# A fused attention, MoE and MLP kernel: the x sums of the first MoE pass made in eight parts during attention and parked in DRAM

## The chip, the cores and the metric

The kernel runs on one core of a Trainium2 chip. The time is the device time of one execution in microseconds (us). A core has a matrix engine (PE), three element-wise engines (DVE, ACT, POOL), a sequencer that issues transfers (SP), and 16 DMA engines that all transfers of the kernel share. The on-chip memory of a core is SBUF; matmul results go to eight banks of PSUM.

## The reference

Three stages follow each other. Batch B=4, heads H=8, 512 local and 32 global tokens per batch, head size 64, so x has 2304 rows of 512.

```python
s_ll = where(|i - j| <= 32, q_l @ k_l.T / sqrt(64), -1e9)     # local tokens: a window
a_l  = softmax(concat([q_l @ k_g.T / sqrt(64), s_ll]))        # and the 32 global ones
out_l = a_l @ concat([v_g, v_l])
out_g = softmax(q_g @ concat([k_g, k_l]).T / sqrt(64)) @ concat([v_g, v_l])
x = heads side by side                                        # [2304, 512]

P = exp(x @ w_gate - max)                                     # [2304, 8]
8 times: P /= P.sum(1); P /= P.sum(0); P *= 2304 / 8          # Sinkhorn
y = sum over 8 experts e of  P[:, e] * (relu(x @ w1[e]) @ w2[e])   # 512 -> 1024 -> 512

z = elu(y @ w_in) @ w_out                                     # 512 -> 2048 -> 512
```

## The kernel before

**Arithmetic.** Each fp32 product is three matmuls on rounded halves: high by high, low by high, high by low (`three`, L110). So every operand exists as a pair, with h and l at the end of its name: the high part is a cast (mostly on ACT), the low part the difference (on DVE or POOL).

**Attention.** The loop `for t in range(nq + 2)` (L527) goes over 32 heads, four steps `i` each. Head t is loaded two heads ahead (`load`: kq on SP, L184), split by `prep` (kh on ACT L210, sq and kl on POOL), scored (`s`), exponentiated on ACT (`e`, L254), transposed (`ptp`, copied to `pt`) and multiplied with the values (`o`, L317); DVE copies `o` to `os` (L337), which frees the bank that the next head's `o` needs. Global scores are `sg` (L275), global values `pg`/`og`. Every fourth head 256 columns of x are transposed into the x operands, and from t=21 on `x_out` (L390) writes the pair `xdh`, `xdl` of a batch to DRAM, 1 MB each.

**Filler.** Between the steps PE runs matmuls of a generator, `fill`: gate logits (`lgp`, `lgt`) and the MoE units 0 and 1 on the first 1024 tokens, in plain form (L112 to L121: `m1` products, `hh` by ACT, `hl` by DVE, then `m2` products added into `acc`). Their raw weights are loaded at L458 and split at L104 and L108. Where the filler isn't ready there are `idle` matmuls during the first eight heads (L493).

**First MoE pass.** A unit is half an expert, 16 in all. After the loop the rest of `fill` is worked off in a loop at L1020, and then units 2 to 15 run over the first 1024 tokens. `mix1` makes its products with seven block products `q1` to `q7` in place of eight (`PROD`): they multiply blocks x11, x12, x21, x22 of x and sums s1 to s4 of these with blocks and sums `wt1` to `wt4` of the weights. `mix2` multiplies the result with the second weights and adds it, times P, into eight `acc` tiles. The block x21 lies in the tile `xs4` (named s4 in the code) until unit 1 has used it last; then the sum s4 goes there. `sums_of_x` makes s1 to s4 on POOL, DVE and ACT, a step at every fifth step of the loop at L1020, followed by the load of unit 2's weights (`w1r`, L725) and its first weight sums (`build[:9]`).

**Sinkhorn** is a queue `timed` of nine small pieces, of which `passed(ns)` starts the next one when the matmuls issued since the last are worth its due time. A round is eight DVE instructions (L852 to L845) around one tiny PE matmul `pcs` (L850), which waits for DVE's `cs`. P (`pr`) is first needed at the first finished tile of unit 2's `mix2`; the sums of units 0 and 1 in `acc` are multiplied by P there (L1002, on ACT, eight tiles in a block).

**Order.** All engines work off their own list in the order in which the code issues. A transfer is issued by SP in that order too, and waits there for its source and its destination.

Of the kernel before, what the change touches and what calls it, by code (L numbers as in the profile page):

```python
# [50 lines left out]
def tile_net(ctx: ExitStack, tc, kq, vw, vc, qg, wg, w1, w2, wi, wo, consts, out):  # L51
# [16 lines left out]
    xd = {p: dram.tile([128, 4, TP[1]], F32, tag="xd" + p, name="xd" + p) for p in "hl"}  # L68
    sd = {p: dram.tile([128, 4, 2, HALF], F32, tag="sd" + p, name="sd" + p) for p in "hl"}
    yd = dram.tile([128, TP[0] // 128, D], F32, tag="yd", name="yd")  # L70
    wd = {
# [380 lines left out]
    def load_unit(u):  # L452

        raw = []
        for i in range(10):
# [6 lines left out]
            yield  # L462

    def ready(b):
        while not st.get(("xready", b)):
            yield "wait"
# [11 lines left out]
    with tc.manual_schedule():  # L478
# [46 lines left out]
        prep(0)  # L525
        unit0_weights = load_unit(0)
        for t in range(nq + 2):  # L527
            if t + 2 < nq:
# [11 lines left out]
            for i in range(4):  # L540
# [20 lines left out]
                if i >= 2:  # L561
                    between = scores_g(t, i - 2) if t < nq else iter(())
                    if 0 <= t - 1 < nq:
                        pv(t - 1, i - 2, between)
                    for _ in between:
                        pass
# [9 lines left out]
                if i == 3 and t < nq:  # L576
                    fill_for(FILL)
                    st["gq"] = t

# [6 lines left out]
                if i == 2 and t >= 5 and (t - 5) % 4 == 0:  # L586
                    fill_for(FILL)
                    x_t((t - 5) // 4)
                    if ((t - 5) // 4) % 2 == 1:
                        st["xready", (t - 5) // 8] = True  # L590
                        if (t - 5) // 8 >= 2:
                            x_out((t - 5) // 8)
                if t == 3 * H + 2 and i % 2 == 0:
                    logits_part(2)
        x_tg()
        x_out(B)
        for b in (B - 1, B):
            for _ in range(2):
                logits_part(b)
                for _ in range(9):  # L600
                    next(fill, None)
# [7 lines left out]
    sm = mright.enter_context(tc.tile_pool(name="sm", bufs=1, side="right", reuse_waits="tile"))  # L609
    psum = ctx.enter_context(tc.tile_pool(name="psum", bufs=8, space=PSUM))  # L610

# [10 lines left out]
    def raw_tile(shape, dt, name):  # L622
        r = rawm.tile([128, 2 * HALF], F32, tag="raw", name=name)
        n = int(np.prod(shape))
        v = r[:, :n].bitcast(dt)
        return v.rearrange("p (a f) -> p a f", a=shape[0])

    def second_x(names):
# [10 lines left out]
    def sums_ahead(c):  # L639
# [35 lines left out]
        return [lambda: load("h"), lambda: load("l")], [whole, first, hi, lo]  # L675

    def sums_of_x(m):

        v = {}

        def blk(n, q):
            return xop[n + q][:, :, :m]

        def whole(n, src, eng):
            v[n] = raw_tile((2, m), F32, "x" + n)
            eng.tensor_tensor(out=v[n], in0=blk(src, "h").bitcast(F32), in1=blk(src, "l").bitcast(F32), op=ALU.add)

        def comb(dst, a, b, op, buf):
            nc.vector.tensor_tensor(out=v[buf], in0=v[a], in1=v[b], op=op)
            v[dst] = v[buf]  # L690

        def hi(n):
            nc.scalar.copy(blk(n, "h"), v[n])

        def lo(n, eng=nc.vector):
            eng.tensor_tensor(out=blk(n, "l"), in0=v[n], in1=blk(n, "h").bitcast(F32), op=ALU.subtract)


        eng = nc.gpsimd
        return [  # L700
            lambda: whole("21", "s4", nc.gpsimd),
            lambda: whole("22", "22", nc.vector),
            lambda: comb("s1", "21", "22", ALU.add, "22"),
            lambda: hi("s1"),
            lambda: whole("11", "11", nc.gpsimd),
            lambda: lo("s1", eng),
            lambda: comb("s3", "11", "21", ALU.subtract, "21"),
            lambda: comb("s2", "s1", "11", ALU.subtract, "22"),
            lambda: hi("s2"),
            lambda: hi("s3"),  # L710
            lambda: lo("s2", eng),
            lambda: lo("s3"),
            lambda: whole("12", "12", nc.vector),
            lambda: comb("s4", "12", "s2", ALU.subtract, "12"),
            lambda: hi("s4"),
            lambda: lo("s4"),
        ]

# [225 lines left out]
    def mix2(p, u, i, fcs):  # L944

        if i not in open2:
            open2[i] = [psum.tile([128, 512], F32, tag="b", name="m2"), 0]
        ps, n = open2[i]
        for fc in fcs:
            t = slice(i * 128, i * 128 + 128)  # L950
# [40 lines left out]
    def mix2_all(p, u, last):  # L991
# [7 lines left out]
        rest += [(i, range(4)) for i in range(tiles) if i not in seen]  # L999
        if u == 2 and p == 0:  # L1000
            for i in range(tiles):
                nc.scalar.mul(accs[i], accs[i], pr[:, i, 0:1])  # L1002
        for i, f in pre:
# [8 lines left out]
    with tc.manual_schedule():  # L1012
        conv = deque(range(8 * U2))
        timed.extend(sinkhorn())
        sums = sums_of_x(SL)
        first, build = weights1(2, nc.gpsimd)

        pre = deque(sums[:-2] + first + build[:9])
        steps = 0
        for r in fill:  # L1020
# [3 lines left out]
            passed(r if isinstance(r, float) else 0.0)  # L1024
        pop(pre, len(pre))
        for f in build[9:13]:
            f()
        order = [(0, u) for u in range(2, U1)] + [(1, u) for u in range(U1)]
        nload, nbuild = weights2(2)
        side1.extend(build[13:] + sums[-2:] + nload)  # L1030
        for a, (p, u) in enumerate(order):
# [216 lines left out]
```

## Time and profile before

| | |
|---|---|
| median of 3 runs | 2011.51 us (2010.76 to 2012.47) |
| profiled execution: its own time | 2012.67 us |
| profiled execution: span of the profile | 2010.9 us |
| mean granted PE clock | 0.996 of full |
| busy: PE, DVE, ACT, POOL | 99%, 69%, 37%, 36% |

The 1.77 us between the profiled execution's time and its span lie outside of the program. The attention loop ends at about 256 us, the first product of unit 2 starts at 292.18 us, and from 330 us on PE is busy without a break almost to the end.

### The profile page before, as it was taken

To read this page: it belongs to the slowest core of one execution; us is meant where nothing else is said; L and a number is where in the kernel's file an instruction comes from. 1 tells how busy PE (TensorE), PEld (TensorE's weight loads), DVE (VectorE), ACT (ScalarE), POOL (GpSimd) and SP (SyncE) were. 2 spreads that over 40 slices of the span, in tenths; PEclk is the share of its full clock that TensorE was granted. 3 is DMA by queue.
4 is the path that set the end of the run, shared out by engine and by line. 5 is a ranking of instruction groups with operands and counts; after the bars stand their busy time and mean duration, and the time that the engine had idled before them with its cause. 6 is when DMAs were issued, how large, how long until landed. Compare 5 with 4: busy or idle time off the path is not lost.

```text
span 2010.9 us, 29132 instructions
## 1 busy us (share of the span) xinstructions
PE 1989.8 (99%) x11051; PEld 1739.3 (86%) x11051; DVE 1382.8 (69%) x2531; ACT 752.9 (37%) x1488; POOL 725.9 (36%) x612
## 2 busy tenths in 40 slices
PE   8999999999999999999999999999999999999999
PEld 7998977888888888899999999999999988887997
DVE  6766667677677767777788888888867654445444
ACT  6655524233333323333333333333333233433333
POOL 6554442232243323323344444444423212322222
PEclk9999999999999999999999999999999999999999
DMA  7435331223322232441132232232212140202001
GB/s 230 138 121 160 101 105 53 63 66 103 115 87 90 75 103 85 159 176 63 58 107 93 90 104 85 92 96 86 85 64 73 44 178 1 84 3 81 1 32 58
DMA packets 65628, 181.43 MB, mean 90 GB/s; under 512 B 6608, under 2 KB 16592, under 8 KB 63440
## 3 DMA queue, kind: packets, MB, share of 16 engines
q1 hardware_dynamic: 65488, 179.57, 27.4%
q8 instruction: 87, 1.43, 0.3%
q14 instruction: 53, 0.43, 0.1%
HBM read 146.77 MB, written 32.77 MB: 89 GB/s over the span
## 4 chain that ended last, share of the span: by engine, by line
PE 89%; DVE 4%; ACT 4%; issue 1%; DMA 1%; POOL 0%; SPq 0%; ACTq 0%; DVEq 0%; POOLq 0%
PE m L116 16%; PE m L112 16%; PE m L114 16%; PE q L925 10%; PE q L924 10%; PE q L923 10%; PE o L317 2%; DVE eg L133 2%; PE m L1157 1%; PE m L1156 1%; PE m L1159 1%; PE ptp L300 1%; ACT eg L131 1%; ACT er L132 1%; ACT er L130 1%
## 5 line engine op out<-in xcount | busy, mean ns | idle before, releaser
L116 PE MATMUL m<-w2h,hl 128*128 128x512 f32 x1088 | 428.1, 394 | 2.4 <-DVE hl L121 2.4
L114 PE MATMUL m<-w2l,hh 128*128 128x512 f32 x1088 | 427.6, 393 | 0.0
L112 PE MATMUL m<-w2h,hh 128*128 128x512 f32 x1088 | 427.4, 393 | 0.0
L895 ACT ACTIVATE hh<-t 128x288 fp32r<-128x288 f32 (+1 forms) x368 | 184.9, 502 | 445.5 <-DVE t L892 445.4
L897 DVE SCALAR_TENSOR_TENSOR hl<-t,hh 128x288 fp32r<-128x288 f32 (+1 forms) x368 | 276.4, 751 | 4.0 <-ACT hh L895 0.3
L962 DVE SCALAR_TENSOR_TENSOR acc<-m,pr,acc 128x512 f32<-128x512 f32 x247 | 183.6, 747 | 134.5 <-PE m L116 134.4
L108 POOL TENSOR_TENSOR w2l<-w2r,w2h 128x512 fp32r<-128x512 f32 x120 | 159.5, 1345 | 279.5 <-ACT w2h L104 264.7
L116 PEld LDWEIGHTS m<-w2h,hl 128*128 128x128 f32 x1088 | 204.9, 188 | 44.9 <-DVE hl L121 3.5
L114 PEld LDWEIGHTS m<-w2l,hh 128*128 128x128 f32 x1088 | 205.0, 188 | 41.1
L112 PEld LDWEIGHTS m<-w2h,hh 128*128 128x128 f32 x1088 | 205.2, 189 | 40.4
L892 DVE TENSOR_TENSOR t<-q,u 128x288 f32<-128x288 f32 (+1 forms) x276 | 145.1, 526 | 58.9 <-PE q L925 53.7
L133 DVE SCALAR_TENSOR_TENSOR eg<-eg,er 128x384 f32<-128x384 f32 (+1 forms) x80 | 76.4, 955 | 148.9 <-ACT er L132 148.9
L733 POOL TENSOR_TENSOR wt<-w1r,wt 128x512 f32<-128x512 f32 x60 | 91.5, 1525 | 184.9 <-DVE hl L897 104.2
L733 POOL TENSOR_TENSOR wt<-w1r 128x512 f32<-128x512 f32 x60 | 80.7, 1349 | 178.0 <-DVE hl L897 144.8
L139 POOL TENSOR_SCALAR hh<-eg 128x384 fp32r<-128x384 f32 (+1 forms) x60 | 33.4, 557 | 306.6 <-DVE eg L134 263.9
L737 ACT CAST wh<-wt 128x512 fp32r<-128x512 f32 x120 | 69.4, 618 | 185.5 <-POOL wt L733 185.5
L130 ACT ACTIVATE er<-m 128x384 f32<-128x384 f32 (+1 forms) x80 | 42.8, 535 | 191.9 <-PE m L116 127.7
L808 POOL TENSOR_TENSOR cp<-r,cp 128x512 f32<-128x512 f32 x32 | 44.7, 1397 | 183.3 <-ACT r L807 183.3
L741 DVE TENSOR_TENSOR wl<-wt,wh 128x512 fp32r<-128x512 f32 x116 | 110.7, 972 | 0.0
L906 DVE TENSOR_TENSOR u<-q,s 128x288 f32<-128x288 f32 (+1 forms) x92 | 48.7, 529 | 77.5 <-PE q L925 66.0
L254 ACT ACTIVATE e<-s,m 128x192 f32<-128x192 f32 (+1 forms) x128 | 55.7, 437 | 74.2 <-DVE m L246 73.6
L317 PEld LDWEIGHTS o<-vw,pt 112*128 112x128 f32 x512 | 76.1, 192 | 6.3 <-issue 3.0
(272 smaller groups left out, 5011.2 us busy)
## 6 DMA issues: line engine op xcount, KB each, us to landing
w1r<-in_w_dram SPq DMA_DIRECT2D x60, 512.0 KB, 5.0
w2r<-in_w_dram SPq DMA_DIRECT2D x60, 512.0 KB, 4.4
kq<-in_kq_dram SPq DMA_DIRECT2D x31, 544.0 KB, 3.8
r<-in_wi_dram SPq DMA_DIRECT2D x16, 512.0 KB, 4.0
r<-in_wo_dram SPq DMA_DIRECT2D x16, 512.0 KB, 3.9
vw<-in_vw_dram SPq DMA_DIRECT2D x32, 227.5 KB, 5.1
vc<-in_vc_dram SPq DMA_DIRECT2D x8, 568.8 KB, 4.8
raw<-in_w_dram SPq DMA_DIRECT2D x16, 256.0 KB, 5.0
```

The lines of the kernel that those rows point to most:

```text
L108: e.tensor_tensor(out=lo, in0=src, in1=hi.bitcast(F32), op=ALU.subtract)
L112: nc.tensor.matmul(ps, ah, bh, start=first, stop=False)
L114: nc.tensor.matmul(ps, ah, bl, start=False, stop=False)
L116: nc.tensor.matmul(ps, al, bh, start=False, stop=last)
L733: eng.tensor_tensor(out=t, in0=get(a), in1=get(b), op=op)
L892: nc.vector.tensor_tensor(out=t, in0=ps, in1=rest, op=ALU.add)
L895: nc.scalar.activation(hh, t, AF.Relu)
L897: late.append(lambda: nc.vector.scalar_tensor_tensor(out=hl, in0=t, scalar=0.0, in1=hh.bitcast(F32), op0=ALU.max, op1=ALU.subtract))
L923: nc.tensor.matmul(ps, wh, xh, start=k == 0 and i != 3, stop=False, skip_group_check=True)
L924: nc.tensor.matmul(ps, wh, xl, start=False, stop=False, skip_group_check=True)
L925: nc.tensor.matmul(ps, wl, xh, start=False, stop=k == 1, skip_group_check=True)
L962: nc.vector.scalar_tensor_tensor(out=accs[i], in0=ps, scalar=scale, in1=accs[i], op0=ALU.mult, op1=ALU.add)
```

## The change

1. `first_sums` makes the four sums in eight parts of 128 columns (k of two halves, c of four quarters): four POOL additions of the pair into whole values, four DVE additions and subtractions, one ACT cast, one DVE subtraction, and two transfers of 256 KB to new DRAM tensors `sfh`, `sfl`. One of the 32 steps is issued at each (t, i) with t of at least 18 and i other than 2. The last `acc` tile and 128 free columns of `hh`/`hl` hold a part meanwhile.
2. `first_x` reads the sums back: s2, s3 and s1 (six transfers of 512 KB, `xs2h` to `xs1l`) ahead of unit 2's weights, s4 after unit 1's last use of x21. `sums_of_x` and its two buffers' traffic go.
3. The PSUM pool of the MoE stage gets `reuse_waits="tile"`: a bank waits for the old tile that lay there, not for all old tiles.
4. The global scores of the first head, spread over steps 2 and 3 before, are issued together at the head's end.
5. 14 instead of 9 filler steps stand between the last pieces of the logits.
6. The multiplication of an `acc` tile by P stands ahead of that tile's last `mix2` products, one tile at a time; ahead of the first, what is left of Sinkhorn is issued at once (`while timed`).
7. Unit 2's weight loads and sums are now the only things in the list `pre`, so they are issued from the start of the loop at L1020.

```diff
@@ -67,6 +67,7 @@
+    sf = {p: dram.tile([128, 4, 2, SL], F32, tag="sf" + p, name="sf" + p) for p in "hl"}
@@ -461,6 +462,35 @@
                 split(wA[n + "h"][:, k], wA[n + "l"][:, k], raw[i - 2], lo_eng=("dve", "pool")[i % 2])
             yield
 
+    def first_sums(k, c):
+
+        t = slice(c * 128, c * 128 + 128)
+        v = accs[-1].rearrange("p (a f) -> p a f", a=4)
+        g = [hs[p][:, :, 2 * SL:2 * SL + 128] for p in "hl"]
+
+        def whole():
+            for i, n in enumerate(("11", "12", "s4", "22")):
+                h, l = (xop[n + p][:, k, t].bitcast(F32) for p in "hl")
+                nc.gpsimd.tensor_tensor(out=v[:, i], in0=h, in1=l, op=ALU.add)
+
+        def sums():
+            x11, x12, x21, x22 = (v[:, i] for i in range(4))
+            for o, a, b, op in (
+                (x22, x21, x22, ALU.add), (x21, x11, x21, ALU.subtract),
+                (x11, x22, x11, ALU.subtract), (x12, x12, x11, ALU.subtract),
+            ):
+                nc.vector.tensor_tensor(out=o, in0=a, in1=b, op=op)
+
+        def hi():
+            nc.scalar.copy(g[0], v)
+
+        def lo():
+            nc.vector.tensor_tensor(out=g[1], in0=v, in1=g[0].bitcast(F32), op=ALU.subtract)
+            for q in range(2):
+                nc.sync.dma_start(sf["hl"[q]][:, :, k, t], g[q].bitcast(F32))
+
+        return [whole, sums, hi, lo]
+
     def ready(b):
         while not st.get(("xready", b)):
             yield "wait"
@@ -524,6 +554,7 @@
                 nc.gpsimd.memset(e[:, i, WIDTHS[i]:], 0.0)
         prep(0)
         unit0_weights = load_unit(0)
+        ahead = deque(f for k in range(2) for c in range(4) for f in first_sums(k, c))
         for t in range(nq + 2):
             if t + 2 < nq:
@@ -559,7 +590,7 @@
                     transp(t - 1, i)
                 fill_for(FILL)
                 if i >= 2:
-                    between = scores_g(t, i - 2) if t < nq else iter(())
+                    between = scores_g(t, i - 2) if 0 < t < nq else iter(())
                     if 0 <= t - 1 < nq:
                         pv(t - 1, i - 2, between)
@@ -575,6 +606,9 @@
                     prep(1)
                 if i == 3 and t < nq:
                     fill_for(FILL)
+                    if t == 0:
+                        for _ in (*scores_g(t, 0), *scores_g(t, 1)):
+                            pass
                     st["gq"] = t
@@ -590,6 +624,8 @@
                         st["xready", (t - 5) // 8] = True
                         if (t - 5) // 8 >= 2:
                             x_out((t - 5) // 8)
+                if t >= 2 * H + 2 and i != 2 and ahead:
+                    ahead.popleft()()
                 if t == 3 * H + 2 and i % 2 == 0:
                     logits_part(2)
@@ -597,7 +633,7 @@
         for b in (B - 1, B):
             for _ in range(2):
                 logits_part(b)
-                for _ in range(9):
+                for _ in range(14):
                     next(fill, None)
 
@@ -607,7 +643,7 @@
     rawm = mleft.enter_context(tc.tile_pool(name="rawm", bufs=4, side="left", reuse_waits="tile"))
     tmp = mright.enter_context(tc.tile_pool(name="tmp", bufs=2, side="right", reuse_waits="tile"))
     sm = mright.enter_context(tc.tile_pool(name="sm", bufs=1, side="right", reuse_waits="tile"))
-    psum = ctx.enter_context(tc.tile_pool(name="psum", bufs=8, space=PSUM))
+    psum = ctx.enter_context(tc.tile_pool(name="psum", bufs=8, space=PSUM, reuse_waits="tile"))
 
     class Banks:
 
@@ -624,6 +660,12 @@
         n = int(np.prod(shape))
         v = r[:, :n].bitcast(dt)
         return v.rearrange("p (a f) -> p a f", a=shape[0])
+
+    def first_x(names):
+
+        for n in names:
+            for q in "hl":
+                nc.sync.dma_start(xop[n + q][:, :, :SL].bitcast(F32), sf[q][:, ("s2", "s4", "s3", "s1").index(n)])
 
     def second_x(names):
@@ -673,48 +715,6 @@
-    def sums_of_x(m):
...
@@ -946,6 +946,10 @@
         if i not in open2:
             open2[i] = [psum.tile([128, 512], F32, tag="b", name="m2"), 0]
         ps, n = open2[i]
+        if u == 2 and p == 0 and n + len(fcs) == 4:
+            while timed:
+                timed.popleft()[1]()
+            nc.scalar.mul(accs[i], accs[i], pr[:, i, 0:1])
         for fc in fcs:
             t = slice(i * 128, i * 128 + 128)
@@ -997,9 +1001,6 @@
             pre, mid, rest = [(0, range(4))], [], [(1, range(4)), (5, range(4))]
         seen = {i for i, _ in pre + mid + rest}
         rest += [(i, range(4)) for i in range(tiles) if i not in seen]
-        if u == 2 and p == 0:
-            for i in range(tiles):
-                nc.scalar.mul(accs[i], accs[i], pr[:, i, 0:1])
         for i, f in pre:
             mix2(p, u, i, f)
@@ -1012,10 +1013,10 @@
     with tc.manual_schedule():
         conv = deque(range(8 * U2))
         timed.extend(sinkhorn())
-        sums = sums_of_x(SL)
+        first_x(("s2", "s3", "s1"))
         first, build = weights1(2, nc.gpsimd)
 
-        pre = deque(sums[:-2] + first + build[:9])
+        pre = deque(first + build[:9])
         steps = 0
         for r in fill:
             steps += 1
@@ -1023,11 +1024,12 @@
                 pop(pre)
             passed(r if isinstance(r, float) else 0.0)
         pop(pre, len(pre))
+        first_x(("s4",))
         for f in build[9:13]:
             f()
         order = [(0, u) for u in range(2, U1)] + [(1, u) for u in range(U1)]
         nload, nbuild = weights2(2)
-        side1.extend(build[13:] + sums[-2:] + nload)
+        side1.extend(build[13:] + nload)
         for a, (p, u) in enumerate(order):
             after = order[a + 1] if a + 1 < len(order) else None
             switch = after is not None and after[0] != p
```

Three places show how this moves the work. First SP's list in the attention loop, at the writing of batch 2 of x (`xdh`, `xdl`) and the load of head 28 (`kq`). Before:

```order
L390 DMA xdh<-hh 512x1x512
L390 DMA xdl<-hl 512x1x512
L458 DMA raw<-in_w_dram 128x512
L184 DMA kq<-in_kq_dram 128x1088
L458 DMA raw<-in_w_dram 128x512
L194 DMA vw<-in_vw_dram 112x520
```

and with the change:

```order
L391 DMA xdh<-hh 512x1x512
L391 DMA xdl<-hl 512x1x512
L459 DMA raw<-in_w_dram 128x512
L490 DMA sfh<-hh 512x1x128
L490 DMA sfl<-hl 512x1x128
L185 DMA kq<-in_kq_dram 128x1088
L459 DMA raw<-in_w_dram 128x512
L195 DMA vw<-in_vw_dram 112x520
```

Two stores of a part now stand between the x stores and head 28's load. Then ACT's list around the last evacuations `hh` of unit 1 in the loop at L1020 (`m1_...` is the bank that is read, `wt2` a weight sum that POOL makes). Before:

```order
L120 ACTIVATE hh_97<-m1_3747 128x256
L120 ACTIVATE hh_97<-m1_3776 128x256
L120 ACTIVATE hh_97<-m1_3796 128x256
L737 CAST wh_95<-w1r_3792 128x512
L120 ACTIVATE hh_97<-m1_3815 128x256
L737 CAST wh_95<-w1r_3801 128x512
L737 CAST wh_95<-wt2_3856 128x512
L737 CAST wh_95<-wt1_3808 128x512
```

and with the change:

```order
L832 ACTIVATE pr_68<-lg_67,nm_3818 128x136
L737 CAST wh_97<-w1r_3800 128x512
L737 CAST wh_97<-w1r_3807 128x512
L121 ACTIVATE hh_99<-m1_3848 128x256
L737 CAST wh_97<-wt2_3860 128x512
L121 ACTIVATE hh_99<-m1_3866 128x256
L121 ACTIVATE hh_99<-m1_3884 128x256
L121 ACTIVATE hh_99<-m1_3911 128x256
L737 CAST wh_97<-wt1_3814 128x512
```

The last four `hh` now stand behind two casts of `w1r` and three of them behind the cast of `wt2` as well. On DVE a whole Sinkhorn round stands between the `hl` of `m1_3866` and those of `m1_3884` and `m1_3911`, and ahead of them no sum of x any more. Last, DVE's list at the end of Sinkhorn (`t`, `u`, `hl` are evacuations of `mix1`). Before:

```order
L845 TENSOR_REDUCE cs_4091<-pr_68 128x8
L892 TENSOR_TENSOR t_4093<-q4_4074,u3_4061 128x512
L897 SCALAR_TENSOR_TENSOR hl_98<-t_4070,hh_97 128x512
L897 SCALAR_TENSOR_TENSOR hl_98<-t_4093,hh_97 128x512
L852 TENSOR_SCALAR pcs_4130<-pcs_4130 128x8
L853 RECIPROCAL pcs_4130<-pcs_4130 128x8
L854 SCALAR_TENSOR_TENSOR pr_68<-pr_68,pcs_4130 128x136
L892 TENSOR_TENSOR t_4138<-q5_4063,u2_4017 128x512
L962 SCALAR_TENSOR_TENSOR acc4_105<-m2_4106,pr_68,acc4_105 128x512
```

and with the change:

```order
L852 TENSOR_SCALAR pcs_4184<-pcs_4184 128x8
L853 RECIPROCAL pcs_4184<-pcs_4184 128x8
L854 SCALAR_TENSOR_TENSOR pr_68<-pr_68,pcs_4184 128x136
L838 TENSOR_REDUCE rs_4189<-pr_68 128x17
L839 TENSOR_SCALAR rs_4189<-rs_4189 128x17
L840 RECIPROCAL rs_4189<-rs_4189 128x17
L841 TENSOR_TENSOR pr_68<-pr_68,rs_4189 128x136
L845 TENSOR_REDUCE cs_4194<-pr_68 128x8
L892 TENSOR_TENSOR t_4211<-q5_4137,u2_4105 128x512
L852 TENSOR_SCALAR pcs_4214<-pcs_4214 128x8
L853 RECIPROCAL pcs_4214<-pcs_4214 128x8
```

Sinkhorn now ends one full round later in the program: the round of `pcs_4184` stands ahead of the evacuation `t_4211`, which corresponds to `t_4138` of before, and on PE the last two `pcs` are 14 matmuls apart, where two neighbours were 20 to 22 apart.

## Rows read from the trace of the kernel before

**Rows 1.** What PE waited for, whole span: total us, times, longest.
```profile
PE sg L275 <- POOL sqg L224: 2.6, 1, 2.6
...
PE m L116 <- DVE hl L121: 2.4, 2, 1.9
...
PE pcs L850 <- DVE cs L845: 1.8, 1, 1.8
...
PE m L112 <- DVE hl L121: 0.9, 1, 0.9
PE lgt L413 <- DVE acc L447: 0.7, 1, 0.7
```
**Rows 2.** Stretches: us, busy of PE, PEld, DVE, ACT, POOL (instructions), PEclk, DMA share, GB/s.
```profile
10.00:20.00 10.00, 9.79 (x56) 8.84 (x57) 5.54 (x22) 5.90 (x16) 8.32 (x9) 0.68 0.86 266
202.40:211.25 8.85, 6.87 (x61) 6.70 (x60) 5.39 (x18) 5.04 (x13) 5.17 (x5) 1.00 0.76 230
260.00:292.20 32.20, 28.09 (x170) 23.74 (x169) 22.61 (x49) 9.44 (x19) 14.37 (x10) 0.95 0.38 128
282.10:289.70 7.60, 5.21 (x17) 3.40 (x17) 6.44 (x14) 1.62 (x4) 5.01 (x5) 0.78 0.49 167
310.40:316.90 6.50, 4.71 (x15) 3.41 (x15) 6.04 (x17) 1.26 (x2) 2.25 (x2) 0.74 0.57 165
330.00:1000.00 670.00, 670.00 (x3157) 564.25 (x3156) 472.45 (x708) 215.13 (x389) 209.57 (x156) 1.00 0.29 94
```
**Rows 3.** Chain of waits, then timelines, 194 to 209 us: start us, us, what [idle before <-releaser].
```profile
194.29 9.22 DMA kq<-in_kq_dram
...
203.61 0.67 ACT L210 CAST kh<-kq 128x576 fp32r<-128x576 f32 x1 [1.04 <-DMA kq<-in_kq_dram]
...
208.18 0.41 DVE L337 COPY os<-o 128x260 f32<-128x260 f32 x1
...
208.69 0.41 PE L317 MATMUL o<-vw,pt 112*128 112x65 f32 x2 [1.98 <-issue]
```
**Rows 4.** Last x stores: issues on SP, then KB and us from issue to landing.
```profile
257.86 0.52 SPq L390 DMA_DIRECT2D xdl<-hl  x1
...
259.95 1.38 SPq L390 DMA_DIRECT2D xdl<-hl  x1
...
xdl<-hl SPq DMA_DIRECT2D x1, 1024.0 KB, 6.9
...
xdl<-hl SPq DMA_DIRECT2D x1, 256.0 KB, 7.7
```
**Rows 5.** First and last of twelve back-to-back loads: SP issues, then us to landing.
```profile
839.46 0.38 SPq L637 DMA_DIRECT2D x11h<-xdh  x1
...
849.06 0.37 SPq L637 DMA_DIRECT2D x22l<-xdl  x1
...
x11h<-xdh SPq DMA_DIRECT2D x1, 576.0 KB, 4.7
...
x22l<-xdl SPq DMA_DIRECT2D x1, 576.0 KB, 11.7
```
**Rows 6.** Timelines of PE, POOL and ACT at the start of unit 2.
```profile
285.44 0.50 PE L116 MATMUL m<-w2h,hl 128*128 128x512 f32 x1 [1.94 <-DVE hl L121]
...
292.18 0.40 PE L923 MATMUL q<-x11h,wh 128*128 128x512 f32 x1
...
285.30 1.28 POOL L733 TENSOR_TENSOR wt<-w1r 128x512 f32<-128x512 f32 x1 [2.59 <-DMA w1r<-in_w_dram]
...
289.08 1.66 ACT L737 CAST wh<-wt 128x512 fp32r<-128x512 f32 x3 [3.21 <-POOL wt L733]
```
**Rows 7.** Timeline of DVE, 300 to 313 us: xs4's sum, a Sinkhorn round's ends.
```profile
300.61 1.23 DVE L696 TENSOR_TENSOR xs4l<-x,xs4h 128x1024 fp32r<-128x1024 f32 x1 [1.10 <-ACT xs4h L693]
...
310.21 0.16 DVE L852 TENSOR_SCALAR pcs<-pcs 128x8 f32<-128x8 f32 x1
...
312.19 0.40 DVE L845 TENSOR_REDUCE cs<-pr 128x8 f32<-128x136 f32 x1
```

More of the change, by code (lines that the diff above doesn't have):

```diff
@@ L675, in sums_ahead @@
         return [lambda: load("h"), lambda: load("l")], [whole, first, hi, lo]
-    def sums_of_x(m):
[L679 to L717, printed above, removed]
     def weights1(u, eng=nc.vector):
```

## The prediction, made before the result was known

> **What bounds the kernel now.** I read the waits of PE first [rows 1], then the stretches around each wait [rows 2], then the engine timelines there, and the DMA issues last. The reader is to see that the waits are few and all early: from 330 us on PE has no gap at all at full clock [rows 2], and in that part every engine's order stays as it was. So only the first 330 us can change. There PE waits once at the start for the split global queries (2.6 us) [rows 1], once at 208 us for an `o` bank (2.0) [rows 3], then for the logits (0.7), for unit 1's `hl` (0.9, then 1.9 and 0.5), and for Sinkhorn's `cs` (1.8) [rows 1]. A wait can cost more than its length. After the first, the 10 us stretch ran at a mean clock of 0.68, and around the two of the transition it was 0.78 over 7.60 us and 0.74 over 6.50 us [rows 2]: 0.22 × 7.60 = 1.7 us and 0.26 × 6.50 = 1.7 us lost to the 1.2 GHz level. After the wait of 2.0 us at 208 us the clock stayed at 1.00 [rows 2]. So a wait of 2 us stands near the edge of a clock loss of 1.7 us.
>
> The transition has the largest loss: of the 32.20 us from 260 to 292.2 us PE worked 28.09 [rows 2]. 4.1 us of gaps and 1.7 us of low clock, 5.8 us, is the most that a perfect transition up to unit 2's first product gives.
>
> **The start.** One idle matmul goes ahead of the global scores, into the 2.6 us wait for the split queries, which stays. A matmul there costs between 0.2 us (670.00 us for 3157 matmuls at full clock) and double that at half clock [rows 2]. I take −0.4, since the stretch ran slow; the ends are 0 and −2.0, if the later scores let the clock recover sooner.
>
> **The sums in attention.** Of 128 columns each, a part's work is four POOL additions (1.28 us for 512 columns [rows 6], a quarter each: 1.3 us in all), four DVE operations (128x1024 takes 1.23 us and a 128x136 reduction 0.40 [rows 7]: between 0.15 and 0.40 each, 0.6 to 1.6 us), one DVE subtraction of 512 columns (half of 1.23, 0.6), one ACT cast (1.66 us for three: 0.55 [rows 6]). In the busiest head that I looked at, 202.40 to 211.25 us, DVE worked 5.39 of 8.85 us, ACT 5.04, POOL 5.17 [rows 2]; a part comes every 1.3 heads, so each of them has the idle time for it. I take 0.3 us for collisions, with ends 0 and 8 × 1.9 = 15 us (DVE's share of every part lands on PE).
>
> The stores do not hide as well. At 194 us the DMA engines are busy with 2 MB of x, and `kq` of head 28 takes 9.22 us to land; ACT waits for it, then `kh`, the casts behind it on ACT, DVE's subtraction, and DVE's `os` at 208.18 are late one after the other, and PE waits 1.98 us for that copy [rows 3]. (The profile names no releaser; `os` frees the bank.) Exactly there two stores of 256 KB in pieces of 512 bytes now stand ahead of `kq`. The nearest row is the same kind of pair at the end of attention: the 1 MB ahead landed at 257.86 + 6.9 = 264.8 us, the second 256 KB at 259.95 + 7.7 = 267.7: 2.9 us for the pair [rows 4]. Contiguous loads bound it below: eleven of 576 KB took (849.06 + 11.7) − (839.46 + 4.7) = 16.6 us, 1.51 each [rows 5], so 512 KB 1.3 us. I take 2.4, nearer to the stores of the same shape, whose figure holds an end in which nothing followed. It lands on PE one for one, since PE is already waiting: a wait of 4.4 us, over the edge. For the clock I take 1.0 of the 1.7 us. Attention: 0.3 + 2.4 + 1.0 = +3.7.
>
> **The transition.** With the four sums gone DVE no longer works on them while `hl` waits. If nothing else is late, unit 2's first product comes 5.8 us sooner, at 292.2 − 5.8 = 286.4 us by the old clock. The kernel pays for it with a new queue: SP now issues six loads of 512 KB ahead of `w1r`. One of them goes ahead of the x stores, five behind. The x stores are in at 267.7 us [rows 4], then seven transfers (five loads and `w1r` twice) at 1.51 × 512 / 576 = 1.34 us each [rows 5] end at 277.0 us. From `w1r`'s landing, POOL's two `wt` with a subtraction between them, and the cast of `wt2` on ACT took 289.08 − 285.30 = 3.8 us [rows 6], so the cast begins at 280.8 us. In the new ACT list three `hh` stand behind it. 0.6 for the cast, 0.4 for `hh_3866` and 0.4 for its `hl`; then on DVE the round that was put ahead of `hl_3884`, 312.19 + 0.40 − 310.21 = 2.4 us [rows 7]: `hl_3884` comes at about 284.5 us. When does PE want it? Before, the late `hl` released PE at 285.44 and the first product followed at 292.18 [rows 6], 6.7 us later, of which 0.5 was the second wait and 1.7 low clock: 4.5 us of work. So it wants it at 286.4 − 4.5 = 281.9. The wait is 2.6 us, with ends 0.6 and 4.6 for `w1r` 2 us sooner or later, and with a clock loss of 1.5 (0 to 1.7) because it is longer than the 1.9 that lost the clock there. Transition: −5.8 + 2.6 + 1.5 = −1.7.
>
> The Trainium skill has a slower rate for this: its page "SBUF — State Buffer", section "Summary: rules for kernel authors", has one reckon about 358 GB/s for transfers between DRAM and SBUF. By that the seven transfers would take 10.3 us, not 9.4, and the sum would be 0.9 us higher. This trace doesn't agree: twelve loads ran at 590 KB in 1.51 us, 391 GB/s [rows 5].
>
> **Sinkhorn.** Before, the wait for `cs` cost 1.8 and 1.7 us of clock. The sum s4 (1.23 us on DVE after 1.10 us of waiting for its cast [rows 7], 2.3 together) no longer stands ahead of it, which is more than the wait. But the queue starts later and its end is forced ahead of the first finished tile: the last two `pcs` are 14 matmuls apart, not 22, which takes 8 × 0.22 = 1.8 us of DVE's time away. 1.8 − 2.3 + 1.8 = 1.3 us of wait stay at the last `pcs`, and with the clock 3.0 against 3.5: −0.5. The ends: −3.5 if the wait goes, +1.0 if POOL's weight work doubles two DVE operations.
>
> **At nothing.** The `acc` multiplications block no one on PE now ([rows 1] name no wait for them), and one at a time are hidden likewise. The banks' own waits: of the 4.1 us of gaps from 260 to 292.2 us, the waits for `hl` and the logits are 2.4 + 0.9 + 0.7 = 4.0 [rows 1], which leaves a bank 0.1. Five more filler steps fill time that PE would spend on the same matmuls later. s4's load has the first products of unit 2 as cover (1.6 us in all if that were gone).
>
> **The sum.** −0.4 + 3.7 − 1.7 − 0.5 = +1.1 us on the profiled execution's 2012.67: 2013.8. That execution is 1.2 us above the median, so against the median of 2011.51 it is 2012.6. A difference below 0.2%, 4.0 us, can't be told from none here.
>
> **The rivals.** *Both queues are short enough* (faster). The loads are in before `wt2` is wanted and `kq` is not delayed. For it: the wait for `hl` goes if `w1r` lands 2.6 us before my 277.0, the end of a reckoning over 20 us. Against it: 9.22 us for `kq` shows how full the engines are. Then −0.4 + 0.3 − 5.8 − 3.5 = −9.4: 2002.1 us. *Only head 28 is late*: −0.4 + 3.7 − 5.8 − 0.5 = −3.0: 2008.5. *Only unit 2's weights are late*: −0.4 + 0.3 − 1.7 − 0.5 = −2.3: 2009.2. *The parts aren't hidden* (slower). Each part stands in DVE's and POOL's lists ahead of `os`, `z` and the next head's `kl`, and 11 heads run through it; DVE is free 3.5 of 8.85 us [rows 2], but not when it is wanted. It decides from 0.4 us a part on: 8 × 0.4 = 3.2 and the 1.1 of the sum pass 4.0. At 0.8 us, 40% of DVE's 1.9, it is 6.4 − 0.3 more: 2018.7. For it: PE's matmuls in attention are short and wait for DVE and ACT in turn. Against it: in the same stretch ACT and POOL too are free for 3.7 us, and a part needs 0.55 and 1.3.
>
> **How the numbers follow.** Both late as reckoned 0.32 (own range 2009.5 to 2015.5), only head 28 0.16, only the weights 0.14, neither 0.18, parts not hidden 0.20. The likeliest is the first: 2012.6. The range drops the outer half of the two far cases, 0.09 and 0.10: 2002.5 to 2018.5. Faster than 2007.5: all of "neither", a third of "only head 28" and a quarter of "only the weights": 0.18 + 0.05 + 0.04 = 0.27. Slower than 2015.5: nine tenths of "not hidden" and a sixth of the first: 0.18 + 0.06 = 0.24. The rest 0.49.
>
> **What would show it.** In the new profile: PE's wait at `o` near 208 us grown from 2.0 to about 4.4 us with `kq`'s landing time at 11 to 12 us; the second `w1r` landing near 277 us; PE's wait for `hl` at 1 to 4 us with ACT's `hh` behind the cast of `wt`; the first product of unit 2 near 292 us, 1 to 3 us sooner or later by the sum of these; one wait at the last `pcs`. I am wrong if `kq` of head 28 lands as before, if `w1r` lands by 274 us, or if the waits of PE before 190 us grow.

## The result and the profile after

The changed kernel is slower, by 0.6%. It took a median of 2024.99 us (2022.74 to 2025.86, six runs) against 2012.35 (2010.76 to 2013.38, six runs): the ratio is 1.0062 with a 95% interval of 1.005 to 1.0075. The prediction was 2012.6 with a range up to 2018.5, so it was wrong: the time lies 6.5 us beyond the range. The profiled execution of the changed kernel has a span of 2024.0 us, 13.1 more than before.

The list of PE's waits in the changed kernel shows what is new (total us, times, longest):

```profile
PE ptp L301 <- DVE pt L308: 4.1, 4, 2.0
PE ptp L301 <- ACT pt L306: 3.7, 3, 2.6
PE m L113 <- ACT hh L137: 2.2, 7, 0.6
PE pcs L850 <- DVE cs L845: 1.8, 1, 1.8
PE o L318 <- issue: 1.8, 2, 1.0
PE sg L276 <- POOL sqg L225: 1.7, 1, 1.7
PE m L117 <- DVE hl L122: 1.7, 1, 1.7
PE m L113 <- DVE lg L417: 1.6, 1, 1.6
```

Most waits of [rows 1] are still there; the one for the first queries is 1.7 us, not 2.6, and the ones for `hl` at the end of unit 1 are 1.7, not 2.4. New are the transposes `ptp`, which wait for `pt` of the attention loop: 7.8 us, longest 2.6, where before had 1.2. The stretches behind the longest ones are slow as well (columns as in [rows 2]):

```profile
135.00:140.00 5.00, 3.18 (x16) 3.03 (x17) 3.95 (x15) 3.58 (x8) 1.41 (x1) 0.69 0.19 53
140.00:145.00 5.00, 5.00 (x32) 5.00 (x31) 1.94 (x8) 0.94 (x2) 2.86 (x7) 0.63 0.88 271
...
210.00:215.00 5.00, 4.02 (x23) 4.02 (x24) 4.23 (x16) 3.31 (x7) 2.60 (x3) 0.69 0.94 278
...
230.00:235.00 5.00, 5.00 (x42) 4.59 (x43) 3.63 (x13) 2.91 (x7) 4.50 (x5) 0.76 0.53 160
```

In these four stretches alone the low clock cost up to (0.31 + 0.37 + 0.31 + 0.24) × 5 = 6 us (less where PE also stood still).

To see where the 13.1 us came from I set markers in both traces. DVE copies `o` to `os` once a head; the copy that ends head 16 stands ahead of the first part's sums, the one of head 31 behind the last. In the changed kernel:

```profile
131.09 0.43 DVE L338 COPY os<-o 128x260 f32<-128x260 f32 x1 [0.65 <-PE o L318]
...
269.06 0.43 DVE L338 COPY os<-o 128x260 f32<-128x260 f32 x1 [1.29 <-PE o L318]
...
306.25 0.40 PE L923 MATMUL q<-x11h,wh 128*128 128x512 f32 x1
```

Before, the first product stood at 292.18 us [rows 6], and the two copies here:

```profile
133.27 0.43 DVE L337 COPY os<-o 128x260 f32<-128x260 f32 x1 [0.65 <-PE o L317]
...
254.16 0.43 DVE L337 COPY os<-o 128x260 f32<-128x260 f32 x1 [1.29 <-PE o L317]
```

So the start was 2.2 us faster, the heads with parts took 17.1 us more, the transition 0.8 less, and all behind it 1.0 less (13.1 in all, by the spans, less 14.1 at the first product). The prediction had −0.4, +3.7, −1.7 and −0.5 for the four. The attention term, +3.7, is the one that failed.

What happens there is plainest in the last of the eight parts. First come the scores that wait for a mask, then DVE, POOL, ACT and PE:

```profile
221.57 0.28 PE L236 MATMUL s<-kl,sq 128*128 128x192 f32 x1
...
222.61 0.20 DVE L280 TENSOR_SCALAR mg<-mg 32x1 f32<-32x1 f32 x1
222.74 2.26 DVE L482 TENSOR_TENSOR acc<-acc 128x128 f32<-128x128 f32 x3
225.03 1.46 DVE L482 TENSOR_TENSOR acc<-acc 128x128 f32<-128x128 f32 x1
226.41 0.35 DVE L247 CUSTOM_DVE_ANT_0 s<-s,masks 128x192 f32<-128x192 f32 x1
...
222.80 0.69 POOL L210 TENSOR_SCALAR sq<-kq 128x512 fp32r<-128x512 f32 x1
223.57 1.27 POOL L212 TENSOR_TENSOR sq<-kq,sq 64x512 fp32r<-64x512 f32 x1
224.92 1.42 POOL L216 TENSOR_TENSOR kl<-kq,kh 128x576 fp32r<-128x576 f32 x1
...
226.57 0.62 ACT L485 CAST hh<-acc 128x512 fp32r<-128x512 f32 x1 [2.88 <-issue]
227.35 0.42 ACT L255 ACTIVATE e<-s,m 128x192 f32<-128x192 f32 x1 [0.17 <-DVE m L247]
228.18 0.59 ACT L306 COPY pt<-ptp 112x512 f32<-112x512 f32 x1
...
228.82 0.53 PE L301 MATMUL ptp<-ident,e 128*112 128x128 f32 x2 [2.61 <-ACT pt L306]
```

The four additions of 128x128 took 3.75 us; the fourth alone took 1.46 and ended 0.15 us after POOL's `kl`. In DVE's list they stand ahead of the mask of these scores. DVE was free for it from 222.8 us, and it started at 226.41, 3.6 us later. On ACT the part's own cast `hh` came as late and stands ahead of the exponential. The exponential, the copy `pt` and PE's transposes follow one another from there, and PE stood still for 2.6 us.

The parts are not alike. The first (at 132 us) and the fifth (181 us) are stretched like this one. In three others one addition took 0.65 to 0.69 us. In the two at 158 and 193 us none took over 0.30, and the heads around these two (19 and 20, 23 and 24) took no longer than in x1_nosums, which makes no sums.

### The profile page after: what moved, and what is told of

It reads as the page before. It is cut to its first block, busy times and chain, and to the rows that moved or that the text cites. A ratio compares the mean times of both kernels' runs of the same rounds, so it can differ in the third digit from the quotient of the medians.

```text
span 2024.0 us, 29238 instructions
## 1 busy us (share of the span) xinstructions
PE 1995.2 (99%) x11051; PEld 1742.7 (86%) x11051; DVE 1393.5 (69%) x2563; ACT 752.7 (37%) x1492; POOL 730.7 (36%) x640
## 4 chain that ended last, share of the span: by engine, by line
PE 88%; DVE 5%; ACT 4%; POOL 1%; issue 1%; DMA 1%; SPq 0%; ACTq 0%; DVEq 0%; POOLq 0%
PE m L117 16%; PE m L113 16%; PE m L115 16%; PE q L925 10%; PE q L924 10%; PE q L923 10%; PE o L318 2%; DVE eg L134 2%; PE m L1159 1%; PE m L1158 1%; PE m L1161 1%; PE ptp L301 1%; ACT er L133 1%; ACT eg L132 1%; ACT er L131 1%
```

## The experiments

The times of single runs stand beside a run of the kernel before on the same chip. The table gives the four terms for each kernel's profiled execution, worked out from the three markers and the span, as differences from before in us. Each row is one execution. Single runs of the kernel before lie between 2010.2 and 2014.8 us, and x3_stores and x6_start, which have the old code from the loop's end on, stand at +2.0 and +1.9 in the transition and at −0.5 and −1.0 in the rest. So a difference of up to 2 us in one cell need not be the edit's. x3_stores has the old code at the start, and its start is 1.7 us faster too; that is taken up at x6_start.

| kernel | start | attention | transition | rest | span |
|---|---|---|---|---|---|
| the change | −2.2 | +17.1 | −0.8 | −1.0 | +13.1 |
| x1_nosums | −0.8 | +3.0 | −0.8 | −0.8 | +0.6 |
| x2_reduce | −1.4 | +5.8 | −0.8 | −0.4 | +3.2 |
| x3_stores | −1.7 | +3.6 | +2.0 | −0.5 | +3.4 |
| x4_pool | −1.0 | +5.0 | −0.8 | −0.7 | +2.5 |
| x5_spread | −1.4 | +7.9 | −2.2 | −1.0 | +3.4 |
| x6_start | −1.5 | +1.5 | +1.9 | −1.0 | +0.9 |
| x7_w1first | −2.3 | +16.5 | −5.1 | +1.0 | +10.1 |
| x8_best | −1.1 | +5.7 | −5.1 | −0.6 | −1.1 |
| x9_clear | −1.8 | +2.5 | +2.6 | −1.2 | +2.1 |
| x10_early | −1.7 | +9.1 | −5.1 | −1.3 | +1.0 |
| x11_two | −1.4 | +2.0 | −5.2 | −0.7 | −5.2 |

**x1_nosums**: the sums left out.

```diff
         def sums():
             x11, x12, x21, x22 = (v[:, i] for i in range(4))
-            for o, a, b, op in (
...
-                nc.vector.tensor_tensor(out=o, in0=a, in1=b, op=op)
+            return
```

> The changed kernel without the four DVE additions and subtractions of each part (the stored values are then the whole blocks, not their sums); POOL's additions, the ACT cast, the low part on DVE and all stores stay. Theory DVE (the sums stand in DVE's list ahead of the next scores' masks and delay exp, transposes and PE): most of the 17 us that attention got longer goes, to 3 to 6 us, time near 2012. Theory stores (the transfers delay head 28's load and others): nothing changes, 2024 to 2026.

It took 2013.32 us beside 2010.41 for before. Of attention's 17.1 us 3.0 are left. Without the four DVE operations of each part 14.1 us are gone, 1.8 a part in the mean, though they are 1.2 us of work. Up to 5 us of it are clock: by stretches of 5 us the changed kernel's attention lost 6.8 us to the low clock (the four stretches above and two smaller ones), this kernel's 1.7.

**x2_reduce**: as much work on DVE, but with one SBUF operand.

```diff
-                nc.vector.tensor_tensor(out=o, in0=a, in1=b, op=op)
+            for o in (x22, x21, x11, x12):
+                nc.vector.tensor_reduce(out=o[:, 0:1], in_=o, axis=AX.X, op=ALU.max)
```

> The changed kernel with each of the four DVE additions and subtractions of a part replaced by a reduction of 128x128 with one operand in SBUF (the stored values are not the sums). Theory port (DVE operations with two SBUF operands wait while POOL works, so the 32 sums take 16.6 us and not 9.4): the reductions take about 0.3 us each, none above 0.4, and the attention part loses 6 to 10 us of its 17. Theory DVE's own work (1.2 us a part is enough, and its waiting for POOL's additions): at most 3 us better.

2015.91 beside 2010.41; attention lost 11.3 of its 17.1 us. Grouped by line, from 125 to 240 us, the additions of the changed kernel and the reductions of this one (busy us, mean ns, idle before):

```profile
L482 DVE TENSOR_TENSOR acc<-acc 128x128 f32<-128x128 f32 x32 | 16.6, 520 | 3.2 <-POOL acc L474 2.4
```

```profile
L479 DVE TENSOR_REDUCE acc<-acc 128x1 f32<-128x128 f32 x32 | 6.8, 273 | 2.4 <-POOL acc L474 2.4
```

Both wait 2.4 us for POOL's whole values. The reductions are not stretched; the additions, 293 ns in the median, are, up to 1461. The 19 additions that ran beside no POOL instruction took 281 to 294 ns, the 13 that ran beside one 854 in the mean. From x1 to x2 attention grew by 2.8 us: DVE's own work, its wait for POOL, and 1.7 us more of low clock. The other 11.3 us, more than the 6 to 10 expected, go with the two-operand form: 32 × 247 ns = 7.9 us more of DVE's time, the masks behind it, and a low clock that cost up to 6.8 us in attention, not 3.4. This is what the Trainium skill says on its page "SBUF — State Buffer", section "Who interferes with whom": a DVE instruction with two inputs in SBUF contends with a POOL instruction that reads SBUF, since its second input comes through a read interface that the two share. The trace agrees: 520 ns against 273, and the 1.46 us addition that ended just after `kl`. The prediction did not weigh it for the sums.

**x3_stores**: the kernel before with the sixteen stores alone.

```diff
+                if t >= 2 * H + 2 and i != 2 and ahead:
+                    c = ahead.popleft()
+                    if c is not None:
+                        k, c = divmod(c, 4)
+                        for p in "hl":
+                            nc.sync.dma_start(sf[p][:, :, k, c * 128:c * 128 + 128], hs[p][:, :, 2 * SL:2 * SL + 128].bitcast(F32))
```

> The kernel before with only the sixteen stores of 256 KB added at their places in SP's list (of zeros that POOL writes once), and no part of the sums. Theory stores, as predicted: head 28's load lands 2.4 us later and attention grows by 3 to 4 us, to 2015 or 2016. Theory DVE: within 1 us of before.

2016.07 beside 2010.41, and attention 3.6 us longer, all of it between the `os` copies of heads 24 and 27. The x store, the lines that answer to [rows 3], and the two stretches behind:

```profile
189.67 0.53 SPq L391 DMA_DIRECT2D xdh<-hh  x1
...
195.30 1.80 SPq L185 DMA_DIRECT2D kq<-in_kq_dram  x1
...
kq<-in_kq_dram SPq DMA_DIRECT2D x1, 544.0 KB, 7.7
...
207.94 0.66 PE L318 MATMUL o<-vw,pt 112*128 112x65 f32 x2 [2.49 <-DVE os L338]
...
205.00:210.00 5.00, 2.51 (x14) 2.34 (x13) 2.71 (x10) 2.04 (x5) 2.16 (x3) 0.69 1.08 316
210.00:215.00 5.00, 5.00 (x31) 5.00 (x31) 2.75 (x10) 3.40 (x8) 3.70 (x4) 0.63 0.87 270
```

Before, the x store was issued here:

```profile
191.40 0.60 SPq L390 DMA_DIRECT2D xdh<-hh  x1
```

The load of head 28 is issued 5.6 us after the x store at 189.67, against 2.9 before. But it landed 7.7 us after its issue, not 9.2 [rows 3]: 13.3 us after the x store against 12.1, so 1.2 us late and not 2.4. PE's wait at `o` grew only from 1.98 to 2.49 us, but now the clock fell, up to (0.31 + 0.37) × 5 = 3.4 us. Before lost none there; x6_start, which has no stores, lost 1.7 us of clock at this place and 1.5 us of attention. So the predicted mechanism exists, half as large in the load and a fifth as large in the wait, and beyond what x6_start lost some 2 of the 3.6 us are left for the stores, by this one comparison. That the whole comes near the predicted 3.4 is luck. It is not what made the change slow.

**x4_pool**: the sums on POOL.

```diff
-                nc.vector.tensor_tensor(out=o, in0=a, in1=b, op=op)
+                nc.gpsimd.tensor_tensor(out=o, in0=a, in1=b, op=op)
```

> The changed kernel with the four additions and subtractions of each part on POOL, not DVE. Theory DVE and port: DVE is late only by its 0.7 us for the low part, so the masks come in time and attention loses 9 to 15 of the 17 us, time 2010 to 2016. Theory POOL (its list, with the next head's kl in it, is as tight as DVE's): the wait moves to s behind kl, and the time stays over 2020.

2015.13 beside 2010.41: 12.1 of attention's 17.1 us gone, with the whole computation done. On POOL 128x128 takes 458 ns in the median and 464 at most. POOL's list has more room at these places than DVE's. What makes up the 5.0 us that stay was not split; the part's low part `hl` on DVE, also an operation with two SBUF operands, now took 1.15 us in the median and up to 1.82 (0.68 and 1.67 with the change).

**x5_spread**: the sums on DVE one by one, a step each.

```diff
-        return [whole, sums, hi, lo]
+        return [whole, *sums, hi, lo]
...
-                if t >= 2 * H + 2 and i != 2 and ahead:
+                if t >= 2 * H + 2 and ahead:
```

> The changed kernel with the four DVE sums of a part issued one by one, a step of the loop each, and at all four steps of a head (a part is then seven steps). Theory port and block: a single sum delays the masks by at most one POOL instruction, 1.3 us, not by 3 or 4, so attention loses 6 to 12 us of its 17. Theory DVE's total work: the same 17 us, since the same instructions run.

2016.1 us. The 32 additions take 13.1 us instead of 16.6, still stretched, but attention loses 9.2 of its 17.1 us: no mask stands behind four of them at once. So the same instructions cost about half as much in another place; it isn't DVE's total work. The edit also moves the stores: head 28's load is issued 2.8 us after the x store again, so not all of the gain need be the sums'.

**x6_start**: the kernel before with only the first head's scores moved.

```diff
-                    between = scores_g(t, i - 2) if t < nq else iter(())
+                    between = scores_g(t, i - 2) if 0 < t < nq else iter(())
...
+                    if t == 0:
+                        for _ in (*scores_g(t, 0), *scores_g(t, 1)):
+                            pass
```

> The kernel before with only the first head's global scores moved together. If the 2.2 us by which the changed kernel's profile is ahead at the start is the edit's, the time falls by 1.5 to 2.5 us, to about 2010. If it is the arrival of the first queries, which differs from run to run, the time is within 1 us of before.

2012.45 us (ten runs) against 2012.13 (21 runs), ratio 1.0001 with an interval of 0.9992 to 1.001: no gain. The start in the trace is 1.5 us faster, but in x3_stores, which has the old start, it is 1.7 us faster as well. So the edit isn't shown to do anything, and the profiled execution of before had a slow start: by stretches of 5 us it lost up to 3.4 us of clock in the first 20 us, x3_stores none. This kernel's later terms show something else. At 207 us PE waits as long as before [rows 3], in a stretch that was at 1.00 before [rows 2]:

```profile
207.12 0.41 PE L317 MATMUL o<-vw,pt 112*128 112x65 f32 x2 [1.93 <-issue]
...
208.00:212.00 4.00, 4.00 (x24) 4.00 (x23) 2.57 (x8) 2.90 (x7) 2.32 (x4) 0.57 0.77 235
...
314.51 0.39 PE L853 MATMUL pcs<-cs,ones 128*128 128x8 f32 x2 [1.81 <-DVE cs L848]
...
308.00:320.00 12.00, 10.00 (x44) 7.62 (x42) 10.32 (x26) 4.83 (x9) 5.46 (x4) 1.00 0.30 89
```

0.43 × 4 = 1.7 us of clock are lost where before nothing was, and the start's lead is gone by head 27. At Sinkhorn it is the other way round: the wait for `cs`, 1.81 us after before's 1.8 [rows 1], now keeps the full clock, where before had 0.74 [rows 2], and the rest is 1.0 us shorter with the old code.

**x7_w1first**: unit 2's weights loaded ahead of the sums.

```diff
-        first_x(("s2", "s3", "s1"))
         first, build = weights1(2, nc.gpsimd)
+        for f in first:
+            f()
+        first_x(("s2", "s3", "s1"))
-        pre = deque(first + build[:9])
+        pre = deque([None, None] + build[:9])
```

> The changed kernel with the load of unit 2's first weights ahead of the sums that are read back, on SP, and nothing else moved. Theory queue, as predicted: the last weights land 6 to 7 us sooner, the wait for hl (1.7 us) and the low clock behind it go, and unit 2 starts 3 to 4 us sooner: 2020 to 2022. If the wait for hl is DVE's own round, not the weights, it stays.

2022.75 us. The transition is 5.1 us shorter than before and 4.3 shorter than with the change, the wait for `hl` at the end of unit 1 and the low clock behind it are gone, and the first product comes 32.9 us after the last `os` copy. POOL has the weights at 284.00, where the changed kernel had to wait until 291.56:

```profile
291.56 2.54 POOL L733 TENSOR_TENSOR wt<-w1r 128x512 f32<-128x512 f32 x2 [20.88 <-DMA w1r<-in_w_dram]
...
296.62 0.62 ACT L737 CAST wh<-wt 128x512 fp32r<-128x512 f32 x1 [3.07 <-POOL wt L733]
...
300.67 0.80 PE L117 MATMUL m<-w2h,hl 128*128 128x512 f32 x1 [1.66 <-DVE hl L122]
```

```profile
284.00 2.54 POOL L733 TENSOR_TENSOR wt<-w1r 128x512 f32<-128x512 f32 x2 [14.04 <-DMA w1r<-in_w_dram]
...
301.27 0.40 PE L923 MATMUL q<-x11h,wh 128*128 128x512 f32 x1
```

The first fence is the changed kernel, the second this one. Its rest is 1.0 us longer than before: at the last `pcs`, after a wait of 1.84 us like the changed kernel's, the clock fell to 0.83 over the 10 us from 325 to 335.

**x8_best**: the sums on POOL, the weights first, and one part's stores a step later. Beside x4's and x7's edits:

```diff
-                if t >= 2 * H + 2 and i != 2 and ahead:
+                if t >= 2 * H + 2 and i != 2 and (t, i) != (3 * H + 1, 3) and ahead:
```

> All three repairs in one: the sums on POOL, unit 2's weights loaded ahead of the sums, and one part's stores held back a step, behind head 28's load. By the terms: attention 5.0 us longer with the sums on POOL, less 3 for the stores; transition 0.8 us shorter, 3.5 more for the weights; Sinkhorn 1 us shorter. Sum about 3 us under before, 2008 to 2010. If the stores cost where they go now, or POOL is late for the next head, the time stays at 2011 to 2014.

2011.61 us (eleven runs) against 2012.13, ratio 0.9998 (0.9989 to 1.0007). The weights gave their 5.1 us; holding the stores back gave nothing that shows (attention 5.7 against x4's 5.0). Head 28's load gained by it, landing 11.46 us after the x store against 13.45 in x4_pool, but from 210 to 220 us the low clock cost 1.7 us that x4_pool did not lose. That expectation failed: the step is only moved, and in the next head ACT stood before the part's cast, waiting 1.10 us for POOL's sum, with the exponentials behind it.

```profile
206.93 0.62 ACT L485 CAST hh<-acc 128x512 fp32r<-128x512 f32 x1 [1.10 <-POOL acc L482]
```

**x9_clear**: no part in heads t = 24 to 27, and POOL's work in steps of two operations. Against x8_best:

```diff
-        return [whole, sums, hi, lo]
+        return [
+            lambda: whole((0, "11"), (1, "12")), lambda: whole((2, "s4"), (3, "22")),
+            lambda: sums((3, 2, 3, ALU.add), (2, 0, 2, ALU.subtract)),
+            lambda: sums((0, 3, 0, ALU.subtract), (1, 1, 0, ALU.subtract)), hi, lo,
+        ]
...
-                if t >= 2 * H + 2 and i != 2 and (t, i) != (3 * H + 1, 3) and ahead:
+                if t >= 2 * H + 2 and not 3 * H <= t < 3 * H + 4 and ahead:
...
+        while ahead:
+            ahead.popleft()()
```

> The repairs once more, with every part kept out of the four heads around the writing of batch 2 of x (t = 24 to 27), where loads, ACT and PE are tight: sums on POOL, two POOL operations a step, six steps a part, at all steps of t = 18 to 23 and from 28 on; unit 2's weights ahead of the sums. If the cost that stayed with the sums on POOL lies in those four heads, attention is at most 1.5 us longer than before, the transition 5 us shorter, the end 0.5 shorter: 2007 to 2009. If it is POOL's and ACT's work anywhere, attention stays 3 to 5 us longer: 2010 to 2012.

2015.01 us against 2011.73, ratio 1.0013 (1.0004 to 1.0022). Attention is down to +2.5, of which 1.5 come at heads 25 to 27, where x6_start lost 1.5 with no part at all. But a new wait of 5.4 us came behind the loop:

```profile
267.18 0.58 PE L113 MATMUL m<-xs4h,wh 128*128 128x256 f32 x1 [5.40 <-ACT lt L409]
...
266.08 0.58 ACT L375 CAST hh<-xtg 128x512 fp32r<-128x512 f32 x1 [7.76 <-DMA sfh<-hh]
```

The last part's stores now went out behind the last batch of x, and the columns that they read are those in which ACT has to put the global tokens' x.

**x10_early**: five steps a part, four POOL additions in the first one, t = 24 to 26 left out. Against x9_clear:

```diff
-            lambda: whole((0, "11"), (1, "12")), lambda: whole((2, "s4"), (3, "22")),
+            lambda: whole((0, "11"), (1, "12"), (2, "s4"), (3, "22")),
...
-                if t >= 2 * H + 2 and not 3 * H <= t < 3 * H + 4 and ahead:
+                if t >= 2 * H + 2 and not 3 * H <= t < 3 * H + 3 and ahead:
...
-        while ahead:
-            ahead.popleft()()
```

> As the run before, but the parts end a head and a half earlier (five steps a part, only t = 24 to 26 left out), so that the last part's stores go out ahead of the last batch of x and release the columns that the global tokens of x need. If the 5.4 us wait for the logits was those stores, it goes: attention at most 1.5 us longer than before, the transition 5 us shorter, the end 0.5 shorter: 2007 to 2009. If another wait takes its place there, 2011 or more.

2014.01 us against 2011.68, ratio 1.0011 (1.0002 to 1.002). The wait behind the loop is gone, but heads 20 to 22 lost 4.5 us where x9 lost next to nothing, and later heads more.

**x11_two**: x9_clear with all of these edits but the first.

> The grain of x9_clear (two POOL operations a step, six steps a part), with t = 24 to 26 left out as in x10_early, so that the last stores still go out ahead of the last batch of x. If x10_early lost its 4.5 us in heads 20 to 22 to four POOL operations in one step, attention is as in x9_clear, 2.5 us longer from the start's gain on, and without x9_clear's wait of 5.4 us unit 2 starts 4 to 5 us sooner than before: 2007 to 2009. If the parts cost the same in whatever grain, attention loses 5 us or more again: 2010 to 2013.

2008.38 us (eleven runs, 2006.41 to 2011.06) against 2012.36 (15 runs): the ratio is 0.9983 with an interval of 0.9974 to 0.9992. This is faster than both kernels: at the medians 4.0 us under before. Its page and its waits:

```profile
span 2005.7 us, 29241 instructions
```

```profile
PE o L318 <- issue: 2.6, 2, 2.0
PE sg L276 <- POOL sqg L225: 2.1, 1, 2.1
...
PE ptp L301 <- DVE pt L308: 1.0, 3, 0.4
```

Of PE's waits behind the loop only the first for `hl`, 0.9 us, is left up to unit 2, and `ptp` waits 1.0 us in all for DVE, 1.2 before. The clock helped: in this execution no stretch of 5 us behind 15 us is below 1.00, where before lost some 1.7 us of clock around 285 us and again around 313 us [rows 2]. Why x10's steps cost so much more than these isn't settled: the steps differ in the number of POOL operations and in the places at which the rest of a part falls, and no run changed one of them alone.

## Why the prediction was wrong

**The sums in attention** is the step that failed. It took "0.3 us for collisions", because each engine had idle time for a part in the busiest head [rows 2]. The DVE sums cost about 14 us (x1_nosums). An engine that is free 3.5 of 8.85 us is free in pieces; its list decides what stands ahead of what, and in the last part the four sums stood ahead of a mask that could have started 3.6 us sooner. The price was off too: 0.15 to 0.40 us an addition holds at 0.29 while no POOL instruction runs beside it, but the mean was 0.52. POOL works on the next head's `sq` and `kl` just there, and DVE's additions waited for it. The waits of PE that followed cost clock as well: up to 5 us of the 14. One of the prediction's own signs of being wrong came true: between 125 and 190 us, where PE's list before shows no wait, PE waited 5.1 us.

The rival "parts aren't hidden" named this and its sign, with 0.20, but at 0.8 us a part; the runs gave 1.8 in the mean. The upper end, 8 × 1.9 = 15 us, stood in the text, and then the range cut it off at the middle of the rival. That 15 comes near 14.1 is luck: it puts DVE's plain work on PE, and the runs had stretched additions and lost clock. Still, a bound that no row excludes belongs in the range.

**The stores**: +3.4 for head 28's delay and its clock. Alone they came with 3.6 (x3_stores), of which 1.5 come without stores as well (x6_start), and with a load that was 1.2 us late, not 2.4. In the changed kernel the load came 1.5 us late and PE's longest wait at `o` was 1.0 us, not 4.4. How much of the 17.1 us they add there was not separated; in x1_nosums, with the stores in place and the sums gone, the heads from 24 on lost 2.1.

**The transition**: predicted −1.7, measured −0.8, with waits of 1.7 us for `hl` and 0.5 for `hh` against 2.6, and a clock of 0.76 over 7 us behind them, 1.7 against 1.5. The mechanism was right: the second `w1r` landed 23.6 us behind head 31's `os` copy, where the prediction had 277.0 − 254.2 = 22.8, and putting the loads first gave 4.3 us, where it had put 2.6 + 1.5 on them. The −5.8 was 0.7 too much: x7_w1first, without these waits and at full clock, gains 5.1, and the first wait for `hl`, 0.9 us, stays in it.

**Sinkhorn**: predicted −0.5, measured −1.0. The wait is as long as before, 1.84 us, not 1.3, but its stretch kept the full clock. That isn't shown to be the change's: x6_start kept it with the old code (−1.0), and x7_w1first lost it with the new one (+1.0). Points 3, 5 and 6 of the change were not run alone.

**The start**: predicted −0.4, measured −2.2 in the trace, and no difference in time from it (x6_start).

## What to carry to other kernels

Work moved into idle time of a busy stage is not priced by the engine's share of that stage: look in the order for the instruction that now stands behind it, and for who waits for that one how soon. An operation with two SBUF operands on DVE beside a busy POOL can cost as much as POOL's instruction: here 1.46 us beside `kl`'s 1.42, not its own 0.29. When a queue gets new loads, what is needed first belongs in it first: that edit alone shortened the transition by 4.3 us, where the removed work had brought 0.8.

## What the runs showed that I had not expected

Whether a wait costs clock isn't decided by its length alone. The same wait at `o`, 1.98 us in one run and 1.93 in another, was followed by a clock of 1.00 [rows 2] and of 0.57 over 4 us. The wait at the last `pcs`, 1.84 us with the change and in x7_w1first, was followed by 1.00 and by 0.83 over 10 us. Around the end of unit 1 the old code lost a clock of 0.66 for 5 us in one run and for 10 us in another, after a first wait of 1.94 and 1.92 us (the second was 0.5 and 1.0). So executions of the same code can differ by some 2 us at one such place, and the prediction's flat 1.0 us for a clock loss at head 28 stood between outcomes of 0, 1.7 and, in x3_stores, up to 3.4. What tells them apart stays open.
